# Two VectorE score blocks in one step, and a new plan, in a fused attention and MLP kernel

## The chip, the cores and the metric

The kernel runs on one core of a Trainium2 chip. The metric is the device time of one execution in microseconds (us): the median of several runs. A core has TensorE (PE, with its weight loads shown apart as PEld), VectorE (DVE), ScalarE (ACT), GpSimd (POOL) and SyncE (SP, whose queue starts DMAs). They run side by side and wait for each other on semaphores. TensorE writes its results to PSUM, here eight banks of 128 x 512 float32.

## The reference

The output is a gated mix of two branches over the same input x (2048 x 640, bf16):

```
g = sigmoid(sum(x * gate_w))
a = softmax(q k^T / sqrt(20)) v @ wo        # 32 heads of 20 columns, 2048 x 2048 scores per head
h = x @ w1 + b1                             # 640 -> 1536
b = (h * tanh(softplus(h))) @ w2            # 1536 -> 640
out = g * a + (1 - g) * b
```

The exponentials of the softmax, 32 x 2048 x 2048 of them, are most of the element-wise work.

## The kernel before, in words

**Tiling.** The 2048 queries are cut into four chunks c of 512, the 32 heads into eight groups g of four heads j, the keys into 16 tiles kt of 128. A unit (c, g, kt, j) is one block of scores, 128 keys x 512 queries; there are 2048. The four heads of a group lie on four strips of 32 partitions, so score matmuls (L1163) of different j use different 32-row strips of TensorE and can run at the same time. The last group of chunk 3 is cut into two halves of 256 queries (CUTS). PV matmuls (L1399) take four blocks of one key tile, one per head, and accumulate in PSUM bank 6 (ACC).

**Two ways to an exponential.** ScalarE takes two blocks of a step in one ACTIVATE (`emit_e`, L1190), written to a ring of 16 slots (ETS); with a third block when `third` allows it. VectorE takes whole tiles of four blocks instead: `x_block` picks a tile, a block of it and a bank, `emit_x` issues the block's score matmul and its evacuation (L1248), which turns the score into an integer whose bits are an approximate float16 exponential, in a "line" (LN, or part of HB, REG or W2R). When a tile's four blocks are there, two shaded copies of the line are made (L1278, 128 x 2048), and the three versions go through PV with three scaled copies of V (VS, made by GpSimd at L1303, `weigh`). A VectorE tile so costs four evacuations, two copies and two more PV passes. `start_tile` starts a tile if VectorE's owed work, the free lines and the blocks left in the group allow it; `able` and `room` (with LOAD, GROUP, CALM, LAG, CATCH_UP) gate it from the step loop.

**PSUM.** Banks 0 to 2 and 3 to 5 are the score slots of even and odd steps (`SLOT` = 3). Step s uses the first two banks of its slot; the third of each (2 and 5) and bank 7 are shared (`FLEX`) by VectorE's blocks, by the third block and by the background tasks (`home`). A bank can be taken when its last reader is done in the plan.

**The order of the work** is planned in Python before anything is issued. `Plan` holds a modelled clock for each engine; each `add` puts an instruction behind its engine's last one, with its dependences, which become semaphore waits. The step loop in `attention` runs a step for each exponential of ScalarE: `emit_e(step)`, then the choice of a VectorE block, `compose` (which units ScalarE takes two steps on, by preference on other strips than the VectorE block's), `emit_s`, `emit_x`, PV (`emit_pv`), background tasks (`pick`, `put`) and VectorE's deferred pieces (`work`):

```
x = x_block(step + 2, able) if fast else None
compose(step + 2, x and x[1][3], third(step + 2, x))
emit_s(step + 2)
if x:
    emit_x(step + 2, *x)
```

Background tasks are the projections to Q, K and V, the MLP (`h_task`, evacuated at L941 and blended at L982 to L984; `b_task`, L998) and the output projection (`p_task`, `part_task`, L1021). Each has a due slot (a slot is three blocks, 683 of them, `NSLOT`); those of the MLP and of the output projection of chunks 0 to 2 are spread from `start` (the first block of chunk 2) to `NSLOT - END`. `fill_up` adds matmuls without use (L1685, `spin`), or repeats score matmuls, when the plan's TensorE was busy for less than a share (SPUN, STREAM) of the last WINDOW us; a matmul in flight keeps the clock that TensorE is granted from falling.

A group ends with its last PV; then bank 6 is copied out (L1486), the sums are inverted and spread by DMA, and GpSimd multiplies (L1456).

## Time and profile before

| | |
|---|---|
| median of 3 runs | 770.0 us (768.5 to 771.22) |
| profiled execution: its own time | 769.53 us |
| its span, first to last instruction | 767.7 us |
| mean granted TensorE clock | 0.994 of full |
| DMA | 50.41 MB, mean 66 GB/s |

Durations in the text come from the profiled execution. Two things help to read it. "PE busy" counts matmuls that overlap in a pipeline, so it isn't TensorE's load; a group of matmuls on different strips shows as several records that start within a few ns. And an instruction's duration contains a latency that the next one on the same engine can overlap, so the time that an engine needs per instruction is read from start to start. A row of a view by operation has: line, engine, operation, output <- input, shapes, count | busy us, mean ns of one | idle us just before, and whom that waited for. A row of waits has: who <- whom: us in total, times, longest. A row of the busy time by stretch has: start:end, length, then the busy us (and instructions) of each engine, granted clock, share of the DMA engines busy, GB/s. A timeline row has: start, length, engine, line, operation, count.

### The profile page before, as it was taken

What the parts mean: (1) busy time and instruction counts of PE and PEld (TensorE: products, weight loads), DVE (VectorE), ACT (ScalarE), POOL (GpSimd) and SP (SyncE); (2) the same over time, 40 slices, a digit from 0 to 9 for tenths busy, and PEclk for the clock granted to TensorE, in tenths of its full rate; (3) what the DMA queues carried; (4) which work ended last, traced back from release to release, by engine and by line L of the source; (5) the groups of instructions that cost most, each with busy time, mean ns of one, the idle gap of its engine ahead of it and who ended that gap; (6) DMA issues with size and microseconds to landing.
All of it is one profiled execution on the core that took longest, in us unless ns stands there. A gap on an engine that the chain in (4) does not pass through costs nothing.

```text
span 767.7 us, 25231 instructions
## 1 busy us (share of the span) xinstructions
PE 736.7 (96%) x11185; PEld 277.1 (36%) x11185; DVE 684.9 (89%) x1101; ACT 744.1 (97%) x784; POOL 191.8 (25%) x297
## 2 busy tenths in 40 slices
PE   8999999999999999899999999999999999999995
PEld 3333243333333433223333344433443433332342
DVE  3598899989998999998999899989999999998975
ACT  5999999999999999999999999999999999999994
POOL 3212124223023220223233033311141212324210
PEclk9999999999999999999999999999999999998999
DMA  9423321210234122162212222212222212101001
GB/s 220 70 66 68 100 71 35 64 61 22 73 95 127 54 67 69 51 210 50 59 46 68 58 64 68 51 38 69 66 59 67 66 44 66 34 25 33 16 17 41
DMA packets 78012, 50.41 MB, mean 66 GB/s; under 512 B 21408, under 2 KB 73880, under 8 KB 77848
## 3 DMA queue, kind: packets, MB, share of 16 engines
q1 hardware_dynamic: 75528, 48.24, 23.2%
q8 instruction: 90, 1.47, 0.8%
q10 hardware_dynamic: 2256, 0.47, 0.3%
q0 software_dynamic: 112, 0.01, 0.1%
q14 instruction: 26, 0.21, 0.1%
HBM read 39.01 MB, written 8.90 MB: 62 GB/s over the span
## 4 chain that ended last, share of the span: by engine, by line
ACT 67%; PE 21%; DVE 7%; DMA 3%; SPq 1%; issue 0%
ACT ETS L1190 65%; PE PS L1163 7%; PE PS L1399 6%; PE PS L463 5%; PE PS L807 2%; ACT REG L965 2%; DVE LN L1248 2%; DMA XB<-in_A_x_dram 2%; DVE LN L1278 1%; SPq L512 1%; DMA W2R<-in_B_w_dram 1%; DVE REG L1248 0%; DVE U L983 0%; DVE HB L984 0%; DVE REG L982 0%; PE PS L848 0%
## 5 line engine op out<-in xcount | busy, mean ns | idle before, releaser
L1190 ACT ACTIVATE ETS<-PS 128x1024 bf16<-128x1024 f32 (+1 forms) x753 | 720.9, 1174 | 7.5 <-PE PS L1163 5.9
L1163 PE MATMUL PS<-QT,KT 32*128 32x512 bf16 (+1 forms) x2112 | 295.5, 379 | 17.0 <-ACT ETS L1190 13.8
L1248 DVE TENSOR_SCALAR LN<-PS 128x512 int16<-128x512 f32 x380 | 254.4, 682 | 22.7 <-PE PS L1163 21.4
L1163 PEld LDWEIGHTS PS<-QT,KT 32*128 32x128 bf16 x2112 | 73.9, 91 | 242.6 <-ACT ETS L1190 222.0
L1303 POOL TENSOR_SCALAR VS<-V_all 128x84 bf16<-128x84 bf16 x252 | 140.7, 558 | 83.2 <-DVE V_all L788 34.7
L1456 POOL TENSOR_TENSOR QT<-OUNG,BCT 128x512 bf16<-128x512 f32 x31 | 43.8, 1412 | 465.4 <-DMA BCT<-SUMS 444.8
L1399 PE MATMUL PS<-ETS,V_all 128*21 128x512 bf16 (+1 forms) x1608 | 153.2, 378 | 0.3 <-DVE V_all L788 0.3
L1278 DVE TENSOR_SCALAR LN<-LN 128x2048 int16<-128x2048 int16 x174 | 122.0, 705 | 10.7 <-PE PS L1399 10.1
L463 PE MATMUL PS<-XB,REG 128*32 128x256 bf16 (+1 forms) x1860 | 93.2, 298 | 1.8 <-DMA XB<-in_A_x_dram 0.7
L463 PE MATMUL PS<-W2R,HB 128*32 128x320 bf16 x1536 | 77.2, 302 | 0.2
L1399 PE MATMUL PS<-LN,VS 128*21 128x512 f16 (+1 forms) x784 | 72.9, 377 | 0.6 <-DVE LN L1278 0.6
L1399 PEld LDWEIGHTS PS<-ETS,V_all 128*21 128x21 bf16 x1608 | 39.2, 90 | 61.6 <-issue 55.3
L463 PEld LDWEIGHTS PS<-XB,REG 128*32 128x32 bf16 x1860 | 43.9, 95 | 28.0 <-issue 15.6
L463 PE MATMUL PS<-WOQ,QT 128*32 128x320 bf16 x1024 | 51.4, 300 | 1.2 <-DVE QT L1479 1.2
L463 PEld LDWEIGHTS PS<-W2R,HB 128*32 128x32 bf16 x1536 | 35.8, 96 | 25.4 <-issue 11.7
L1399 PE MATMUL PS<-LN,V_all 128*21 128x512 f16 (+1 forms) x396 | 37.1, 373 | 0.0
L463 PE MATMUL PS<-XB,WOQ 128*32 128x512 bf16 (+2 forms) x440 | 36.5, 382 | 0.0
L941 DVE TENSOR_TENSOR HB<-PS,B1F 128x512 bf16<-128x512 f32 x48 | 32.7, 681 | 0.7 <-PE PS L463 0.4
L1399 PEld LDWEIGHTS PS<-LN,VS 128*21 128x21 bf16 x784 | 17.9, 89 | 37.7 <-issue 22.3
L463 PEld LDWEIGHTS PS<-WOQ,QT 128*32 128x32 bf16 x1024 | 24.4, 96 | 16.2 <-issue 6.3
L1248 DVE TENSOR_SCALAR REG<-PS 128x512 int16<-128x512 f32 x44 | 29.3, 678 | 0.6 <-PE PS L1163 0.4
L1248 DVE TENSOR_SCALAR W2R<-PS 128x512 int16<-128x512 f32 x36 | 24.4, 685 | 4.7 <-PE PS L1163 4.6
(119 smaller groups left out, 517.5 us busy)
## 6 DMA issues: line engine op xcount, KB each, us to landing
REG<-in_B_w_dram SPq DMA_DIRECT2D x36, 320.0 KB, 3.3
BCT<-SUMS SPq DMA_DIRECT2D x31, 256.0 KB
W2R<-in_B_w_dram SPq DMA_DIRECT2D x12, 320.0 KB, 5.7
QT<-QS SPq DMA_DIRECT2D x28, 128.0 KB, 3.4
KT<-KS SPq DMA_DIRECT2D x28, 128.0 KB
KS<-LN SPq DMA_DIRECT2D x16, 128.0 KB, 3.3
QS<-WOQ SPq DMA_DIRECT2D x16, 120.0 KB
W2R<-in_B_w_dram SPq DMA_DIRECT2D x12, 160.0 KB, 3.8
```

The source lines that it names most:

```text
L463: last = e.matmul(to[at + j:at + j + n, :], w[:, j:j + n], x, start=start, stop=stop, tile_position=(0, at + j))
L512: "sp", lambda e: e.dma_start_transpose(xt(c), x_ap[c * CW:(c + 1) * CW, :]), (), f"xt{c}", cost=4.5)]
L807: return lambda e, bank: e.matmul(PS[:, bank, i * n:(i + 1) * n], xt(t // 4)[:, f, t % 4 * P:(t % 4 + 1) * P], WV[:, f, g * HD:g * HD + n] ...
L941: ev = dve(lambda e: e.tensor_tensor(hb, PS[:, bank, :].rearrange("p (i t) -> p i t", i=2), bias, ALU.add), [last, *b1f, *guarded, *b_read ...
L965: ex = pl.add("act", lambda e: e.activation(U, h, AF.Tanh, bias=MXR[:, 3:4], scale=0.5), [ev, u_free[0], m_bias], cost=0.95)
L1163: op = pl.add("pe", lambda e, to=to, g=real(g), tile=tile, j=j, cols=cols, c=c, of_q=of_q: e.matmul(to[:, cols], KT[32 * j:32 * j + 32, g, ...
L1190: e_op[s] = pl.add("act", lambda e: e.activation(RING[:, p:p + n, :], scores(s)[:, 0:n, :], AF.Exp, scale=SCALE), [s_op[s], *(pv_slot[b] f ...
L1248: bank_free[bank] = x_ops[bank] = tile["op"] = dve(lambda e: e.tensor_scalar(dst, PS[:, bank, :], SCALE * ULPS, BASE, ALU.mult, ALU.add), ...
L1278: op = pl.add("dve", lambda e: e.tensor_scalar(to, src, SHADES[n] - SHADES[held], None, ALU.add), [made, *deps], cost=SHADE, port=True)
L1303: weighted[(c, g, k)] = n, [pl.add("pool", lambda e, i=i, n=n, src=src: e.tensor_scalar(VS[:, n, i, :, :], src, WEIGHTS[i + 1], None, ALU. ...
L1399: lasts[n] = pl.add("pe", lambda e, v=v, j=j, src=src[:, cols], of_q=of_q, begin=begin, end=end: e.matmul(PS[32 * j:32 * j + EW, ACC, of_q ...
L1456: oung_free[0] = bc_read[0] = otn_done[(c, g)] = pl.add("pool", lambda e: e.tensor_tensor(otn(c, g), src, BC, ALU.mult), deps, cost=TIMES, ...
```

## The change

A step may take a second VectorE block. After `x_block` has given x, it is called again with `beside` = (x's bank, x's strip). The second call looks at the shared banks other than x's, and gives nothing if VectorE is more than XPAIR = 0.5 us behind ScalarE in the plan or fewer than 32 units are left; otherwise it follows the rules of the first. Its block avoids x's strip if the tile has another one left. `compose` then takes ScalarE's two blocks with both strips marked as used, no third block is allowed, and both are issued, so that the four blocks can lie on four strips.

The plan's numbers are changed too: slack and clearance terms (SLACK, FREE), how far ahead and how late tasks and tiles may be (AHEAD, CATCH_UP, PACKED, ROWED, CALM), the owed work that still lets a tile start (LOAD, GROUP), where the spread background ends (END 75 to 120 slots before the last, SHIFT), and the look back of the fillers (WINDOW).

```diff
-SLACK = 0.219
+SLACK = 0.158
+XPAIR = 0.5
-ROWED = 4
+ROWED = 6
-FREE = 0.209
+FREE = 0.146
-AHEAD = 24
+AHEAD = 26
-CATCH_UP = 372.816
+CATCH_UP = 346.719
-LOAD = 0.823
+LOAD = 0.576
-GROUP = 2.075
+GROUP = 1.453
-END = 75
-SHIFT = 1.348
+END = 120
+SHIFT = 0.944
-WINDOW = 4.9
-CALM = 7
-PACKED = 17
+WINDOW = 3.3
+CALM = 10
+PACKED = 12
...
-        def compose(s, j=None, more=0):
-
-            some, js = [], [j]
+        def compose(s, js=(), more=0):
+
+            some, js = [], list(js)
...
-        def x_block(s, able):
+        def x_block(s, able, beside=None):
...
             homes = [bank for bank in FLEX if bank not in held and not (now["open"] and now["home"] == bank)]
+            if beside:
+                homes = [bank for bank in homes if bank != beside[0]]
+                if max(0.0, pl.now["dve"] - pl.now["act"]) > XPAIR or len(order) < 8 * HG:
+                    return None
...
             js = [v[3] for v in islice(order, HG) if v[:3] == order[0][:3]] if order else []
+            if beside:
+                js = [*js[:1], beside[1]]
             return tile, block_of(tile, js if len(js) <= 2 else []), bank
 
-        def emit_x(s, tile, u, bank):
+        def emit_x(s, tile, u, bank, more=()):
 
             c, g, kt, j = u
-            got = score_mms([(u, PS[:, bank, :])], [bank_free.get(bank), *inputs(u)], [v[3] for v in slots.get(s, ())])
+            got = score_mms([(u, PS[:, bank, :])], [bank_free.get(bank), *inputs(u)], [*more, *(v[3] for v in slots.get(s, ()))])
...
                 x = x_block(step + 2, able) if fast else None
-                compose(step + 2, x and x[1][3], third(step + 2, x))
+                y = x and x_block(step + 2, able, (x[2], x[1][3]))
+                compose(step + 2, [v[1][3] for v in (x, y) if v], 0 if y else third(step + 2, x))
                 emit_s(step + 2)
                 if x:
                     emit_x(step + 2, *x)
+                if y:
+                    emit_x(step + 2, *y, [x[1][3]])
```

## The prediction

> **What bounds the kernel now.** I read the page's totals and chain first, then the busy time of each engine by stretch.
>
> ```profile
> span 767.7 us, 25231 instructions
> ...
> PE 736.7 (96%) x11185; PEld 277.1 (36%) x11185; DVE 684.9 (89%) x1101; ACT 744.1 (97%) x784; POOL 191.8 (25%) x297
> ...
> ACT 67%; PE 21%; DVE 7%; DMA 3%; SPq 1%; issue 0%
> ```
> ```profile
> 20.00:100.00 80.00, 78.26 (x1004) 26.39 (x1001) 65.32 (x111) 79.57 (x88) 13.94 (x27) 1.00 0.32 73
> 100.00:300.00 200.00, 195.79 (x2572) 73.52 (x2573) 184.00 (x308) 197.79 (x209) 50.23 (x83) 1.00 0.23 66
> 300.00:600.00 300.00, 290.19 (x4829) 110.17 (x4824) 280.27 (x432) 299.76 (x311) 75.63 (x111) 1.00 0.25 69
> 600.00:700.00 100.00, 97.86 (x1643) 37.03 (x1631) 98.70 (x152) 99.74 (x109) 26.88 (x36) 1.00 0.16 47
> 700.00:740.00 40.00, 38.48 (x575) 12.77 (x577) 32.84 (x52) 37.42 (x40) 15.28 (x24) 0.91 0.04 12
> ```
>
> The columns of the second view are PE, PEld, DVE, ACT, POOL busy, then the granted clock. ScalarE is full from 20 to 700 us (79.57 + 197.79 + 299.76 + 99.74 of 680, 3.1 us idle), and the chain is mostly its exponentials. VectorE is idle 14.7, 16.0, 19.7, 1.3 and 7.2 us in the five rows, 58.9 in all. So the time falls only if exponentials leave ScalarE, or if its idle time at 700 to 740 us (2.6 us) goes. What it does, and what VectorE takes from it, by operation and form:
>
> ```profile
> L1190 ACT ACTIVATE ETS<-PS 128x1024 bf16<-128x1024 f32 x699 | 660.5, 1142 | 5.3 <-PE PS L1163 4.9 <-PE PS L1399 0.2
> L1248 DVE TENSOR_SCALAR LN<-PS 128x512 int16<-128x512 f32 x380 | 254.4, 682 | 22.7 <-PE PS L1163 21.4
> L1278 DVE TENSOR_SCALAR LN<-LN 128x2048 int16<-128x2048 int16 x174 | 122.0, 705 | 10.7 <-PE PS L1399 10.1
> L1190 ACT ACTIVATE ETS<-PS 128x1536 bf16<-128x1536 f32 x54 | 85.7, 1589 | 2.1 <-PE PS L1399 1.1 <-PE PS L1163 1.0
> L1248 DVE TENSOR_SCALAR REG<-PS 128x512 int16<-128x512 f32 x44 | 29.3, 678 | 0.6 <-PE PS L1163 0.4
> L1248 DVE TENSOR_SCALAR W2R<-PS 128x512 int16<-128x512 f32 x36 | 24.4, 685 | 4.7 <-PE PS L1163 4.6
> L1248 DVE TENSOR_SCALAR HB<-PS 128x512 int16<-128x512 f32 x28 | 18.8, 682 | 2.8 <-PE PS L1163 2.8
> ```
>
> ScalarE takes 2 x 699 + 3 x 54 = 1560 blocks of 128 x 512 and VectorE 380 + 44 + 36 + 28 = 488, together the 2048 that there are. 488 blocks are 122 tiles of four.
>
> **What one tile is worth.** The durations overlap on an engine, so I use start to start, from a run of 20 exponentials and a pair of VectorE's evacuations:
>
> ```profile
> 710.54 18.44 ACT L1190 ACTIVATE ETS<-PS 128x1024 bf16<-128x1024 f32 x20 [0.53 <-PE PS L1163]
> ```
> ```profile
> 723.51 1.28 DVE L1248 TENSOR_SCALAR LN<-PS 128x512 int16<-128x512 f32 x2
> ```
>
> ScalarE: (18.44 - 1.14) / 19 = 0.91 us for two blocks, 0.455 a block, so a tile that leaves it saves 1.82 us. VectorE: 1.28 - 0.68 = 0.60 us a block, and two shaded copies at 0.705: 4 x 0.60 + 1.41 = 3.81 us a tile. A shorter run also takes 1.82 us away from VectorE, so each added tile needs 3.81 + 1.82 = 5.63 us of its idle time.
>
> **The second block (x_block with beside, emit_x twice).** It removes waits of VectorE for a score block: with one block a step it finishes early and the next comes only with the next step's matmuls. The views of who waited for whom, for the whole run and then for 20 to 100 us:
>
> ```profile
> DVE LN L1248 <- PE PS L1163: 21.4, 50, 1.7
> ...
> ACT ETS L1190 <- PE PS L1163: 5.9, 13, 1.0
> ...
> DVE W2R L1248 <- PE PS L1163: 4.6, 6, 1.3
> ...
> DVE HB L1248 <- PE PS L1163: 2.8, 5, 1.9
> ```
> ```profile
> DVE LN L1248 <- PE PS L1163: 4.1, 4, 1.7
> DVE W2R L1248 <- PE PS L1163: 3.3, 4, 1.3
> DVE HB L1248 <- PE PS L1163: 2.8, 5, 1.9
> ```
>
> 28.8 us of VectorE's 58.9 are such waits, and that bounds what pairs can give: 28.8 / 5.63 = 5.1 tiles, 9.3 us. The other end is nothing. 10.2 us of them lie before 100 us, where tiles are few for other reasons (V and K are still being made); 18.6 are left. A pair also needs a second of the three shared banks, while one is held by whatever background task is open, and VectorE at most 0.5 us behind ScalarE in the plan. I take half of the 18.6: 9.3 / 5.63 = 1.65 tiles, **-3.0 us**. With no x block waiting, VectorE's next late item is a shaded copy that waits for PV to give a line back (10.1 us in the L1278 row above), which pairs don't help.
>
> On TensorE a block more in a step costs little, as two groups of score matmuls show:
>
> ```profile
> 431.02 0.39 PE L1163 MATMUL PS<-QT,KT 32*128 32x512 bf16 x4
> 431.94 0.39 PE L1163 MATMUL PS<-QT,KT 32*128 32x512 bf16 x2
> ```
>
> Four blocks on four rows take the 0.39 us of two. A tile's two more PV passes of four matmuls lie in TensorE's waits for ScalarE. The third block of an exponential, which a pair forbids, is worth nothing: 1589 - 1142 = 447 ns against 455, so losing all 54 costs under half a microsecond. What is queued behind a pair is the evacuation of a background task, 0.60 us later; nothing of ScalarE's waits for it, as its own banks are others.
>
> The Trainium skill speaks against the part: the page "TensorEngine Tiling (Array Packing)", section PSUM Bottleneck, says that tiling speeds up TensorE but not the evacuation of PSUM. The trace agrees, since the two evacuations above are serial at 0.60 us each; where VectorE is full (98.70 of 100 us at 600 to 700) a pair is by that rule worth 0, and the sum would then be without the 3.0.
>
> **The shorter look back (WINDOW 4.9 to 3.3).** The fillers at line 1685 exist to keep TensorE's clock up. Once they did not: busy time by 5 us stretches (the last four columns are POOL, clock, DMA share and GB/s), then TensorE's groups before it (first and last of seven), then two groups that run back to back.
>
> ```profile
> 700.00:705.00 5.00, 4.01 (x27) 0.86 (x25) 4.26 (x6) 5.00 (x6) 4.49 (x5) 0.82 0.06 18
> 705.00:710.00 5.00, 5.00 (x45) 1.10 (x44) 2.72 (x4) 3.28 (x4) 3.54 (x6) 0.50 0.01 3
> 710.00:715.00 5.00, 5.00 (x79) 1.61 (x78) 4.09 (x7) 4.47 (x6) 1.59 (x4) 0.99 0.00 0
> ```
> ```profile
> 699.85 0.39 PE L1163 MATMUL PS<-QT,KT 32*128 32x512 bf16 x2
> ...
> 702.84 0.40 PE L1399 MATMUL PS<-ETS,V_all 128*21 128x512 bf16 x4
> ```
> ```profile
> 715.83 0.40 PE L1399 MATMUL PS<-LN,V_all 128*21 128x512 f16 x4
> 716.05 0.39 PE L1399 MATMUL PS<-ETS,V_all 128*21 128x512 bf16 x4
> ```
>
> The clock was halved for 0.18 x 5 / 0.5 + 5 + 0.1 = 6.9 us, and ScalarE lost 1.72 + 0.53 = 2.25 us. Before it, from 699.85 to 703.44 us, seven groups at 0.22 us (716.05 - 715.83) make 1.54 us, 43% occupancy. A look back of 4.9 us still counts denser work from before the lull; one of 3.3 does not, and adds fillers sooner. Bounds: **-2.25 us**, or nothing gained. I take the gain, since the lull is the kind that a shorter mean sees. The page "TensorE: Matmul & The Clock Gate", Part 1, gives a window of about 3.4 us for this gate, which the 6.9 us fit as two, and calls the window that closes it idle; here 43% was enough to close it, and the measurement decides.
>
> **The plan's other numbers.** CALM 7 to 10 starts tiles three slots, 9 blocks, later: at 488 blocks in 753 steps that is 4.5 x 0.65 = 3 blocks, 0.7 tile, 0 to +1.3 us; I take **+0.7**. END 75 to 120 makes the MLP and projection due 45 slots earlier: the work is the same, so 0 where the tail takes the tiles that the middle gives up (rival C below if not). LOAD 0.823 to 0.576 with GROUP allows 0.576 x 1.1 us for each slot left; with 120 left that is 76 us of owed VectorE work, more than remains then once the background is done, so 0. SLACK, FREE, SHIFT, PACKED, ROWED, AHEAD, CATCH_UP reorder work under ScalarE: 0, with 1 us either way as an estimate from the 3.1 us in which ScalarE idles from 20 to 700 us.
>
> **Sum:** -3.0 - 2.25 + 0.7 = -4.55 us on the profiled execution's 769.53 (span 767.7 and 1.8 around it), 765.0. The median of the runs is 0.5 above it, so 765.4.
>
> **Rivals.** The forecast, **A**, spans all waits filled (770 - 9.3 - 2.25 = 758.5) to 767.7.
>
> **B, no change.** Pairs are rarely taken, since a background task holds one of the three banks, or VectorE's idle time is only moved to the shaded copies. For it: 10.1 us of such waits, and 98.70 of 100 us busy late. Against it: the 28.8 us. Tiles stay within one of 122 and the lull comes back in another place: 770, 767.7 to 772.3.
>
> **C, slower: the work that is moved forward is not paid back.** What VectorE does for the background and its densest stretch of tiles (100 to 200 us, lines 1248 and 1190):
>
> ```profile
> L941 DVE TENSOR_TENSOR HB<-PS,B1F 128x512 bf16<-128x512 f32 x48 | 32.7, 681 | 0.7 <-PE PS L463 0.4
> L982 DVE SCALAR_TENSOR_TENSOR REG<-REG 128x1024 f32<-128x1024 f32 x18 | 23.5, 1303 | 1.1 <-ACT REG L965 1.1
> L984 DVE SCALAR_TENSOR_TENSOR HB<-REG,U 128x1024 bf16<-128x1024 f32 x18 | 22.6, 1254 | 0.0
> L983 DVE SCALAR_TENSOR_TENSOR U<-REG,HB 128x1024 f32<-128x1024 f32 x18 | 22.5, 1250 | 0.0
> L998 DVE TENSOR_SCALAR XB<-PS,OMG 128x320 bf16<-128x320 f32 x28 | 15.2, 542 | 1.2 <-PE PS L463 1.2
> ```
> ```profile
> 100.00:200.00 100.00, 51.09 (x77) 1.00 0.18 51
> ```
> ```profile
> 100.00:200.00 100.00, 99.41 (x105) 1.00 0.18 51
> ```
>
> A pair of hidden tasks is 2 x 0.68 + 1.30 + 1.25 + 1.25 = 5.2 us; 18 of them and some 56 small evacuations at 0.54 are 123 us, due over 222 slots where it was 267. At 1.12 us a slot (767.7 / 683) VectorE's share of it rises from 41% to 49%: 8% of 249 us, 20 us or 5 tiles, must move to the tail. The densest stretch so far has 77 / 105 = 0.73 block a step; a VectorE without background could do 0.91 / 0.95 = 0.96, less the groups' own work about 0.9. If the tail stays at 0.73, 55 steps (45 x 1.12 / 0.91) lack 0.17 block each: 9.4 blocks, 2.3 tiles, +4.3 us, and nothing else gained: 774. It decides where the tail's blocks per step stay under 0.9. Against it: that is just where a second block is allowed.
>
> **D, slower by the clock.** In a tail without background TensorE has per step one score group and 0.5 + 0.75 n PV groups for n VectorE blocks: at n = 0.65, 0.22 x 1.99 = 0.44 us of 0.91, 48%; at 0.9, 53%. 43% closed the gate, so it hangs on fillers. Two lulls more than now cost 4.5 us: 774.5.
>
> **How the numbers follow.** A 0.50, B 0.20, C 0.18, D 0.12. This kernel's measurement tells no less than about 0.3% (2.3 us) from no change; by that A is faster, B the same, C and D slower: 0.50, 0.20, 0.30. The time is A's likeliest, 765.4. The range, 758 to 775, goes from A's bound past C and D, with about 1 in 6 left out, mostly above.
>
> **What would show it.** Right: blocks of line 1248 over 488 by 4 to 12 and groups of four score matmuls beside two-block exponentials; VectorE's waits for L1163 near 20 us or under; a clock of 1.00 from 20 to 740 us; ScalarE still full. Wrong: 488 blocks or fewer (B, C; for C fewer from 300 to 600 us and not more after), a halved clock more than once (D), or more than 6 us in which L1190 waits for L1163, which no part of the sum has.

## The result and the profile after

The changed kernel takes **774.3 us** in the median of 14 runs (772.2 to 777.48), where the kernel before, run beside it, takes 770.73 (767.52 to 773.53). The ratio is 1.0045, with a 95% interval of 1.0027 to 1.0063: slower by 0.45%, 3.5 us. The profiled execution took 773.77 us, its span is 772.0, against 769.53 and 767.7. So the profiled executions differ by 4.2 us and show the whole loss.

Two lines of the page of the changed kernel, the totals and the chain that ended last:

```profile
span 772.0 us, 25210 instructions
...
PE 739.4 (96%) x11173; PEld 276.6 (36%) x11176; DVE 687.3 (89%) x1101; ACT 746.5 (97%) x806; POOL 194.1 (25%) x295
...
ACT 50%; PE 31%; DVE 15%; DMA 2%; issue 1%; DVEq 0%; SPq 0%
```

In the chain ScalarE's share fell from 67% to 50%, TensorE's rose from 21% to 31%. The chain is followed back from the last instruction, so this says first that something other than an exponential stands at the end. Busy time by the same stretches as before, and the last 32 us (PE, PEld, DVE, ACT, POOL, then the clock):

```profile
20.00:100.00 80.00, 78.86 (x1026) 27.03 (x1018) 66.65 (x113) 79.68 (x88) 17.90 (x32) 1.00 0.28 73
100.00:300.00 200.00, 195.04 (x2516) 70.99 (x2508) 186.40 (x311) 198.18 (x216) 52.82 (x83) 1.00 0.23 65
300.00:600.00 300.00, 288.57 (x4619) 105.35 (x4612) 281.98 (x439) 298.50 (x321) 78.04 (x115) 1.00 0.24 64
600.00:700.00 100.00, 97.28 (x1672) 38.07 (x1660) 97.29 (x145) 99.25 (x109) 24.32 (x34) 1.00 0.21 59
700.00:740.00 40.00, 38.04 (x639) 14.66 (x640) 32.96 (x52) 39.96 (x44) 12.43 (x17) 1.00 0.06 17
740.00:772.00 32.00, 25.38 (x584) 13.35 (x581) 15.26 (x32) 18.60 (x21) 2.14 (x2) 0.95 0.11 34
```

The last stretch of the kernel before, to its own end:

```profile
740.00:768.00 28.00, 19.16 (x441) 9.43 (x429) 17.01 (x34) 17.64 (x19) 2.52 (x2) 0.94 0.13 38
```

Up to 740 us nothing was lost: ScalarE is as full as before, its idle time at 700 to 740 us is gone (37.42 to 39.96), the clock is 1.00 throughout. The full clock holds for this execution: over the 14, the mean granted clock is 0.991 to 0.999, 0.995 in the median, and 0.998 in the profiled one. The exponentials by form, and VectorE's score blocks:

```profile
L1191 ACT ACTIVATE ETS<-PS 128x1024 bf16<-128x1024 f32 x765 | 711.2, 1119 | 5.0 <-PE PS L1164 4.1
L1255 DVE TENSOR_SCALAR LN<-PS 128x512 int16<-128x512 f32 x376 | 246.7, 678 | 11.9 <-PE PS L1164 11.4
L1255 DVE TENSOR_SCALAR REG<-PS 128x512 int16<-128x512 f32 x56 | 37.2, 680 | 3.3 <-PE PS L1164 3.2
L1255 DVE TENSOR_SCALAR HB<-PS 128x512 int16<-128x512 f32 x32 | 21.2, 681 | 4.2 <-PE PS L1164 4.1
L1191 ACT ACTIVATE ETS<-PS 128x1536 bf16<-128x1536 f32 x10 | 15.3, 1526 | 0.0
L1255 DVE TENSOR_SCALAR W2R<-PS 128x512 int16<-128x512 f32 x24 | 16.0, 680 | 2.4 <-PE PS L1164 2.4
```

376 + 56 + 32 + 24 = 488 blocks, 122 tiles: not one tile more. VectorE's waits for score blocks did fall, from 28.8 to 11.4 + 3.2 + 4.1 + 2.4 = 21.1 us, and counted in the trace, groups of four score matmuls rose from 43 to 91. So pairs are taken, and earlier: 343 of the 488 blocks lie before 500 us, where it was 328. But the last exponential ends at 758.2 us, as before (758.4). ScalarE's last exponentials, before and after:

```profile
751.92 6.46 ACT L1190 ACTIVATE ETS<-PS 128x1536 bf16<-128x1536 f32 x6 [1.08 <-PE PS L1399]
```
```profile
756.20 2.00 ACT L1191 ACTIVATE ETS<-PS 128x1024 bf16<-128x1024 f32 x2
```

**All of the loss of the profiled execution lies behind them:** 9.3 us then, 13.8 us now. Where it comes from shows in two operations of the background, first before, then after (minimum, median and maximum duration in ns, first and last start in us):

```profile
L998 DVE TENSOR_SCALAR XB<-PS,OMG x28: 535/542/552, 380.3 to 734.6; 128x320 bf16<-128x320 f32 x28
...
L1021 DVE SCALAR_TENSOR_TENSOR W2R<-PS,GATE,XB x8: 542/550/551, 737.0 to 756.5; 128x320 f32<-128x320 f32 x8
```
```profile
L999 DVE TENSOR_SCALAR XB<-PS,OMG x28: 531/542/553, 382.7 to 753.1; 128x320 bf16<-128x320 f32 x28
...
L1022 DVE SCALAR_TENSOR_TENSOR W2R<-PS,GATE,XB x8: 540/550/552, 755.7 to 762.9; 128x320 f32<-128x320 f32 x8
```

The first row is the evacuation of the MLP's second product (`b_task`), the second that of the output projection of the last chunk over its first six groups (`part_task`). `part_task` is ready only when all of `b_task` is planned, since it adds to that result and writes over W2's place. The last `b_task` is evacuated 18.5 us later, though END made it due 45 slots earlier, and so of the eight parts, all over by 757.1 us before, six now start behind the last exponential. The chain from there to the output, after and before (start, length, what):

```profile
758.69 4.14 PE PS L464 x116
...
763.46 0.46 PE PS L464 x8
...
763.91 0.46 PE PS L464 x8
...
764.62 1.03 PE PS L464 x24
```
```profile
760.53 0.43 DVE QT L1479
...
761.01 0.48 PE PS L463 x8
```

Before, the end waits for the last group's own normalization (QT at 760.53) and one projection. After, the same normalization is done at 760.47 in the timeline, and the end still has to work through 116 matmuls of parts and the turns of 0.46 us behind them. It is not VectorE that is busy throughout just before: from 740.0 to 758.2 us it is busy for 7.50 us (12.89 before), TensorE for 18.06 (16.82 before), and the late rows of VectorE wait for L464.

### The profile page after: what moved, and what is told of

It reads as the page before. It is cut to its first block, busy times and chain, and to the rows that moved or that the text cites. A ratio compares the mean times of both kernels' runs of the same rounds, so it can differ in the third digit from the quotient of the medians.

```text
span 772.0 us, 25210 instructions
## 1 busy us (share of the span) xinstructions
PE 739.4 (96%) x11173; PEld 276.6 (36%) x11176; DVE 687.3 (89%) x1101; ACT 746.5 (97%) x806; POOL 194.1 (25%) x295
## 4 chain that ended last, share of the span: by engine, by line
ACT 50%; PE 31%; DVE 15%; DMA 2%; issue 1%; DVEq 0%; SPq 0%
ACT ETS L1191 48%; PE PS L1164 11%; PE PS L1406 9%; PE PS L464 8%; DVE LN L1255 5%; DVE LN L1285 3%; PE PS L808 2%; ACT REG L966 1%; PE PS L849 1%; DVE HB L942 1%; DMA RR<-OUNG 1%; DVE U L984 1%; DVE HB L985 1%; DMA LN<-in_A_x_dram 1%; DVE REG L983 1%
## 5 line engine op out<-in xcount | busy, mean ns | idle before, releaser
L1191 ACT ACTIVATE ETS<-PS 128x1024 bf16<-128x1024 f32 x775 | 723.3, 1124 | 5.0 <-PE PS L1164 4.1
L1164 PE MATMUL PS<-QT,KT 32*128 32x512 bf16 (+1 forms) x2114 | 304.1, 378 | 17.5 <-ACT ETS L1191 13.0
L1255 DVE TENSOR_SCALAR LN<-PS 128x512 int16<-128x512 f32 x376 | 246.7, 678 | 11.9 <-PE PS L1164 11.4
L1310 POOL TENSOR_SCALAR VS<-V_all 128x84 bf16<-128x84 bf16 x250 | 144.5, 578 | 91.2 <-DVE V_all L789 26.6
L1164 PEld LDWEIGHTS PS<-QT,KT 32*128 32x128 bf16 x2114 | 75.8, 91 | 251.7 <-ACT ETS L1191 221.4
L1285 DVE TENSOR_SCALAR LN<-LN 128x2048 int16<-128x2048 int16 x176 | 126.2, 721 | 10.6 <-PE PS L1406 9.9
L464 PE MATMUL PS<-XB,REG 128*32 128x256 bf16 (+1 forms) x1860 | 96.4, 298 | 0.8 <-DVE LN L1255 0.6
L464 PE MATMUL PS<-W2R,HB 128*32 128x320 bf16 x1536 | 75.4, 301 | 1.5 <-DVE LN L1255 1.1
L464 PEld LDWEIGHTS PS<-XB,REG 128*32 128x32 bf16 x1860 | 43.3, 95 | 27.9 <-issue 16.9
L464 PE MATMUL PS<-WOQ,QT 128*32 128x320 bf16 x1024 | 48.6, 300 | 0.4 <-issue 0.3
L464 PEld LDWEIGHTS PS<-W2R,HB 128*32 128x32 bf16 x1536 | 35.7, 96 | 25.1 <-issue 11.6
L1255 DVE TENSOR_SCALAR REG<-PS 128x512 int16<-128x512 f32 x56 | 37.2, 680 | 3.3 <-PE PS L1164 3.2
L464 PE MATMUL PS<-XB,WOQ 128*32 128x512 bf16 (+2 forms) x440 | 36.6, 381 | 0.0
L464 PEld LDWEIGHTS PS<-WOQ,QT 128*32 128x32 bf16 x1024 | 24.2, 96 | 14.8 <-issue 6.2
L1493 DVE COPY OUNG<-PS 128x512 f32<-128x512 f32 x31 | 21.2, 684 | 5.6 <-PE PS L1406 5.4
```

Source lines behind the costliest of these rows:

```text
L464: last = e.matmul(to[at + j:at + j + n, :], w[:, j:j + n], x, start=start, stop=stop, tile_position=(0, at + j))
L1164: op = pl.add("pe", lambda e, to=to, g=real(g), tile=tile, j=j, cols=cols, c=c, of_q=of_q: e.matmul(to[:, cols], KT[32 * j:32 * j + 32, g, ...
L1191: e_op[s] = pl.add("act", lambda e: e.activation(RING[:, p:p + n, :], scores(s)[:, 0:n, :], AF.Exp, scale=SCALE), [s_op[s], *(pv_slot[b] f ...
L1255: bank_free[bank] = x_ops[bank] = tile["op"] = dve(lambda e: e.tensor_scalar(dst, PS[:, bank, :], SCALE * ULPS, BASE, ALU.mult, ALU.add), ...
L1285: op = pl.add("dve", lambda e: e.tensor_scalar(to, src, SHADES[n] - SHADES[held], None, ALU.add), [made, *deps], cost=SHADE, port=True)
L1310: weighted[(c, g, k)] = n, [pl.add("pool", lambda e, i=i, n=n, src=src: e.tensor_scalar(VS[:, n, i, :, :], src, WEIGHTS[i + 1], None, ALU. ...
```

## The experiments

How they were read: for each profiled execution I counted VectorE's blocks and took ScalarE's *work* from the first to the last exponential (0.904 us for one of two blocks and 1.330 for one of three, the medians from start to start before, and its other instructions) and its *idle* time, the rest. That rest also holds what exponentials take beyond these medians: of the 19.0 us before, 7.5 are time without a running instruction. *Last W2* is the start of the last `b_task` evacuation, *tail* the time from the end of the last exponential to the end. The next column counts VectorE's instructions in the tail, three of which are in every kernel the branch, the drain and the semaphore of the program's end. *Halved* is the time before the end of the last exponential in which the trace shows TensorE's clock at half.

The ratios are of all executions, the other columns of one, which can lie off the median: it is the slowest with the lull filled (775.89 us, median 770.71), with FREE (783.62, 780.01), with CALM (776.46, 774.74) and with END 75, and the fastest with short parts (771.26, 774.79), with END 90 and with the pair alone and the copy first.

| kernel | ratio to before, 95% | blocks | work + idle | last W2 | last exp. ends | tail | VectorE instr. | halved |
|---|---|---|---|---|---|---|---|---|
| before | | 488 | 728.0 + 19.0 | 734.6 | 758.4 | 9.3 | 12 | 6.8 |
| after | 1.0045 (1.0027 to 1.0063) | 488 | 729.1 + 17.9 | 753.1 | 758.2 | 13.8 | 20 | 0 |
| after, no pair | 1.0102 (1.0063 to 1.0142) | 476 | 734.0 + 14.8 | 747.6 | 759.9 | 12.9 | 19 | 0 |
| pair alone | 1.0152 (1.0117 to 1.0188) | 508 | 720.2 + 27.5 | 764.6 | 758.8 | 20.7 | 26 | 17.1 |
| pair alone, copy first | 1.0136 (1.0077 to 1.0194) | 508 | 720.1 + 23.7 | 760.8 | 755.3 | 20.8 | 26 | 10.2 |
| before, WINDOW 3.3 | 1.0002 (0.9986 to 1.0019) | 488 | 728.0 + 20.8 | 736.1 | 760.3 | 9.3 | 12 | 6.8 |
| before, lull filled | 0.9993 (0.9971 to 1.0015) | 488 | 728.0 + 26.0 | 741.3 | 765.1 | 8.9 | 12 | 13.7 |
| before, CALM 10 | 1.0054 (1.0031 to 1.0076) | 496 | 724.6 + 21.2 | 759.1 | 757.0 | 17.6 | 23 | 6.8 |
| before, FREE .146 | 1.0118 (1.0086 to 1.0149) | 484 | 730.0 + 29.3 | 719.3 | 769.9 | 11.9 | 15 | 30.7 |
| after, END 75 | 1.0096 (1.0064 to 1.0128) | 496 | 725.5 + 26.5 | 759.7 | 763.1 | 14.0 | 20 | 13.7 |
| after, END 90 | 1.0107 (1.0065 to 1.0148) | 496 | 725.9 + 29.0 | 738.0 | 765.7 | 8.8 | 10 | 3.4 |
| after, short parts | 1.0047 (1.0025 to 1.0070) | 488 | 729.1 + 16.3 | 751.6 | 756.7 | 12.8 | 19 | 0 |
| after, thin tail | 1.0010 (0.9996 to 1.0023) | 488 | 729.1 + 17.5 | 752.9 | 758.0 | 12.5 | 19 | 0.3 |
| pair, other numbers | **0.9948** (0.9931 to 0.9965) | 500 | 724.1 + 16.7 | 729.6 | 751.4 | 12.7 | 17 | 0 |
| the same, no pair | 1.0285 (1.0255 to 1.0315) | 500 | 723.4 + 40.3 | 776.5 | 774.3 | 17.2 | 23 | 23.9 |
| the same, copy first | 0.9947 (0.9926 to 0.9968) | 500 | 724.1 + 16.2 | 729.5 | 751.3 | 12.8 | 17 | 0 |
| pair, third numbers | 1.0069 (1.0046 to 1.0092) | 500 | 723.8 + 27.7 | 741.3 | 762.6 | 11.9 | 15 | 13.7 |

Over the table, *idle* goes with *halved*: 14.8 to 17.9 us where at most 0.3 us is halved, 19.0 to 21.2 where 6.8 are, 23.7 to 27.7 from 10.2 to 17.1, 29.3 and 40.3 above. END 90 is the exception, 29.0 us with 3.4. The table doesn't tell which makes the other, a wait that empties TensorE or a halved clock that makes ScalarE wait.

### The pair and the numbers, each without the other

```diff
-XPAIR = 0.5
+XPAIR = -1
```

> The changed kernel with XPAIR = -1: no step takes two VectorE blocks, all other new numbers stay. The planner now hands VectorE 476 blocks instead of 488. Theory (pairs put VectorE's tiles ahead of the background, and what is left of the background after the last exponential is the loss): the background's last W2 evacuation comes earlier than the changed kernel's 753.1 us and the time from the last exponential to the end falls from 13.8 us to about 10; the last exponential comes some 5 us later (12 blocks at 0.455), so the time is about 773 to 777, no gain, but the loss has changed place. Rival N (the new numbers alone make the loss, the pair is harmless): the stretch after the last exponential stays at 13 us or more and the time is 777 or more.

And the other half, the changed kernel with all the old numbers (XPAIR 0.5 stays):

```diff
-SLACK = 0.158
+SLACK = 0.219
...
-FREE = 0.146
+FREE = 0.209
...
-LOAD = 0.576
+LOAD = 0.823
...
-GROUP = 1.453
+GROUP = 2.075
...
-END = 120
-SHIFT = 0.944
+END = 75
+SHIFT = 1.348
...
-WINDOW = 3.3
-CALM = 10
...
+WINDOW = 4.9
+CALM = 7
...
```

> The changed kernel with all numbers of the plan as before the change: the pair alone. The planner hands VectorE 508 blocks (488 before). Theory: ScalarE has 9 us less to do, but the background is done later by about VectorE's time for the 20 added blocks (5 tiles at 3.8 us, 19 us): last W2 evacuation near 750 us or later where it was 734.6, 13 us or more from the last exponential to the end where it was 9.3, and a time of 773 to 780, slower than before. Rival N: the pair pays as forecast, 762 to 767.

Measured: 776.81 us without the pair, 781.53 with the pair alone, against 770.61 beside them. Both halves are slower than before, and each is slower than the two together. Without the pair the new numbers cost 12 blocks (ScalarE's work rises by 6.0 us, its idle time falls by 4.2) and 3.6 us of tail. That tail of 12.9 us is a miss: about 10 was expected, and 13 or more was the sign of the rival, by which the new numbers alone make the loss. They do make most of the longer tail without any pair. On them the pair wins the 12 blocks back, 4.9 us of work, and 0.57% in the two ratios; a part of the 0.57% is clock, since three of the seven executions without the pair show 0.985 and take 781 to 783 us. With a clock of 0.995 or more the means are 775.6 (four executions) and 773.9 with the pair (ten), 1.7 us. On the old numbers the pair wins 20 blocks, five tiles, 7.8 us of ScalarE's work, and loses more: ScalarE idles 8.5 us more and the tail is 11.4 us longer; the signs are those that were expected, the time is 1.5 us above the range. Two rows of waits of the kernel with the pair alone:

```profile
ACT ETS L1191 <- PE PS L1164: 9.0, 21, 1.1
ACT ETS L1191 <- PE PS L1406: 5.2, 5, 2.0
```

In the kernel before these two rows have 5.9 and 1.3 us. The row of the chain:

```profile
759.53 11.58 PE PS L464 x302
```

302 matmuls of the MLP's second product and of the output projection stand between the last exponential and the end. VectorE's idle time from 20 to 740 us fell only from 58.9 to 47.2, where five tiles at 5.63 us are 28 us. Counted without overlaps, evacuations and copies for the tiles took 15.9 us more in that stretch: 11.6 came out of idle time, the other 4.3 are background that VectorE did not do in it.

### The clock

```diff
-WINDOW = 4.9
+WINDOW = 3.3
```

> The kernel before with WINDOW = 3.3 in place of 4.9 and nothing else. VectorE's and ScalarE's instructions come out the same, in the same order; on TensorE a few fillers move by some groups. The prediction gave the shorter look back 2.25 us, by taking away the halved clock at 703 us. If that holds: clock 1.00 from 690 to 715 us and 768 to 769. Theory now (the lull is a stall of that plan, and fillers in the look back's reach do not cover it): no change, 769.5 to 772, and ScalarE still waits 2 us or more between 700 and 725 us.

And the fillers by force: the score matmuls of the steps at the lull are issued twice.

```diff
-            s_op[s] = score_mms([...], deps)
+            s_op[s] = score_mms([...], deps, times=1 + (fast and 690 <= s <= 706))
```

> The kernel before with the same plan, but the score matmuls of steps 690 to 706 (about 693 to 712 us) are issued twice, so that TensorE is some 65% occupied where it was 43%. If the halved clock at 703 to 710 us cost ScalarE its 2.25 us there: granted clock 1.00 over 690 to 715 us, ScalarE full there, and 767.5 to 769, 1 to 2.5 us under the kernel before. If the stall came from the group's end instead and the clock only followed it: the same idle time of ScalarE and no gain, or a loss of up to 1 us from the added matmuls.

Measured: 771.31 us beside 771.61, and 770.71 beside 770.61: no change in either. Busy time by 5 us stretches, first with WINDOW 3.3 alone, then with the doubled matmuls:

```profile
700.00:705.00 5.00, 2.64 (x28) 0.71 (x25) 3.15 (x6) 4.01 (x5) 2.39 (x3) 0.83 0.17 59
705.00:710.00 5.00, 4.67 (x30) 0.91 (x33) 2.38 (x3) 3.07 (x3) 4.44 (x8) 0.50 0.02 3
```
```profile
705.00:710.00 5.00, 3.57 (x21) 0.61 (x22) 3.96 (x5) 3.29 (x4) 4.60 (x6) 0.71 0.08 21
710.00:715.00 5.00, 5.00 (x39) 0.96 (x38) 1.93 (x3) 2.51 (x3) 2.59 (x6) 0.50 0.00 0
```

With WINDOW 3.3 the lull is there, with 0.83 and 0.50 in the two stretches, where it was 0.82 and 0.50 before, and over the 12 executions the clock is 0.990 to 0.995, as beside them. The shorter look back does not remove it.

With the doubled matmuls the answer is less clear. In the profiled execution the lull is longer and some us later, and 21 matmuls in 5 us show that TensorE had little ready to run. But this is the slowest of 12, with a clock of 0.990. Over the twelve it is 0.996 in the median, against 0.993 in the 22 executions beside them, and six have 0.997 or 0.998. So the lull is probably shorter or absent in many of them, and no trace of such a one was kept. The median is the same all the same, so what the clock wins there the doubled matmuls seem to cost elsewhere: those six take 769.8 us in the mean, and the three executions of the kernel before with 0.997 or 0.998 take 767.1 to 768.6.

What the clock goes with in time shows in the 87 executions of the kernel before that ran beside the experiments. In the mean, 5 with 0.990 take 772.8 us, 34 with 0.993 take 771.1, 14 with 0.995 take 769.8, and 4 with 0.999 take 767.6. The profiled execution of the changed kernel has no lull before the last exponential; since WINDOW alone leaves it, it is something else in that plan. What starts it in the old plan, and what takes it away in the new one, stays open.

### One number alone

```diff
-CALM = 7
+CALM = 10
```

> The kernel before with CALM = 10 in place of 7 and nothing else: no pair; tiles start three slots later. The forecast of the prediction for this number was +0.7 us. Theory (tail set by the background's end, whatever moved it): the planner hands VectorE 496 blocks and puts the last W2 evacuation behind the last exponential's neighbourhood, so a tail of 13 to 17 us and 775 to 780. Rival N2 (only the pair moves the background): within 2 us of the kernel before.

```diff
-FREE = 0.209
+FREE = 0.146
```

> The kernel before with FREE = 0.146 in place of 0.209 and nothing else: VectorE gets 484 blocks, and the background's last W2 evacuation comes some 20 us earlier than in the kernel before. Theory: a tail of about 9 us is the floor (last PV, normalisation, last projections, stores), so the earlier background gains nothing there, and the four blocks fewer put the last exponential 1 to 2 us later: 770 to 773. Rival F (an earlier background keeps shortening the tail): tail under 8 us and 768 or less.

Measured: 774.74 and 780.01 us beside 770.70, so +4.2 and +9.1 us by the ratios, from one number of the plan each. CALM gives eight blocks *more* and a tail of 17.6 us; FREE gives an early background (719.3) and late exponentials (769.9), with ScalarE's row of waits at

```profile
ACT ETS L1190 <- PE PS L1163: 15.2, 22, 1.8
```

where it was 5.9. CALM's signs are about those expected; FREE's time is a miss of 7 us, and its tail is 11.9 where 9 was expected. FREE's added idle time goes with the clock: in its profiled execution five halved stretches, 30.7 us, lie before the last exponential, where the kernel before has 6.8. Of the time in which ScalarE runs nothing, 10.5 of 15.5 us lie in them, against 1.8 of 7.5. Each choice of the plan depends on all before it, so one other choice early gives another plan throughout.

### END: pushed late, or exchanged

```diff
-END = 120
+END = 75
```

> The changed kernel with END back at 75, everything else new: the MLP and projections are due 45 slots later again. Theory (the background ends late because VectorE takes tiles first, wherever its due times lie): the last W2 evacuation stays near 750 (753.1 in the changed kernel, 734.6 before), the tail after the last exponential stays at 12.5 to 15 us, and the median within 4 us of 774. Rival (the new END itself pushed the background to the end): the last W2 evacuation goes back to 735 to 740, the tail to 9 to 10.5 us, and the median to 768 to 771.

```diff
-END = 120
+END = 90
```

> The changed kernel with END 90. By the first theory nothing sets in between and it looks like the changed kernel: last W2 evacuation 748 or later, tail over 12 us. A third theory: the end of the background and the end of the exponentials are exchanged for each other, since both want VectorE and TensorE; then a kernel with an early last W2 evacuation (735 to 740) and a short tail (9.5 to 11 us by the count of what is left) has its last exponential later, at 763 or more, and is no faster than 774.

Measured: 778.43 and 777.93 us beside 769.50. With END 75 the background does not come back to 735: the last W2 evacuation is at 759.7, the tail 14.0. So the new END did not push it late. The theory's sizes were a little short: the evacuation comes 9.7 us later than the 750 that was expected, and the median is 0.4 us beyond the 4 us allowed. With END 90 the background is early, as two rows of its VectorE show, and ScalarE waits instead:

```profile
L999 DVE TENSOR_SCALAR XB<-PS,OMG x28: 535/550/552, 382.2 to 738.0; 128x320 bf16<-128x320 f32 x28
...
L1022 DVE SCALAR_TENSOR_TENSOR W2R<-PS,GATE,XB x8: 541/550/552, 740.9 to 760.1; 128x320 f32<-128x320 f32 x8
```
```profile
ACT ETS L1191 <- PE PS L1406: 10.7, 7, 1.9
```

The tail is 8.8 us, shorter than before, and the last exponential ends at 765.7, 7.3 us later than before. That is as the third theory has it: the end of the background and the end of the exponentials are exchanged. The table is no proof of it. FREE (719.3 and 769.9) and the third set (741.3 and 762.6) also have the background early and the exponentials late, and CALM (759.1 and 757.0) and the pair alone (764.6 and 758.8) the reverse. But FREE's late exponentials go with its halved clock, and with END 75 and with the first set without the pair both ends come late (759.7 and 763.1, 776.5 and 774.3). So the exchange is not shown as a rule.

### What the tail consists of

The first kernel leaves out matmuls of `part_task` (all but the first and the last group), the second also narrows the last chunk's parts and rests to 8 of 320 columns; the plan is that of the changed kernel in both.

```diff
-            return Task([p_mm(c, t, half, g, early) for g in early], HALF * COL, finish, due, ready)
+            return Task([p_mm(c, t, half, g, early) if g in (early[0], early[-1]) else lambda e, bank: None for g in early],
+                        HALF * COL, finish, due, ready)
```

> The changed kernel with the same plan, but of the six groups that the eight partial output projections of the last chunk add up, only the first and the last are multiplied (so the last 512 rows of the output are not the reference's). Theory: the last exponential ends at about 758 as in the changed kernel; of the 148 projection matmuls after it some 60 to 80 are missing, at 0.158 us for four that is 2.4 to 3.2 us, so the time falls to about 771.5. Rival S (ScalarE's lost third blocks and waits make the loss, the matmuls after the last exponential are covered by the last group's normalisation and the stores): within 1 us of the changed kernel.

```diff
...
-                dst, PS[:, bank, 0:HALF], GATE[:, tb:tb + 1], add, ALU.mult, ALU.add), [*deps, *gate_done], HALVED)
+                dst[:, 0:n], PS[:, bank, 0:n], GATE[:, tb:tb + 1], add[:, 0:n], ALU.mult, ALU.add), [*deps, *gate_done], HALVED)
...
```

> The changed kernel with the same plan, but the small tasks that finish the last chunk (eight partial output projections, four remainders) work on 8 of 320 columns, matmul and VectorE evacuation alike, and the partial ones on the first and last of their six groups only (so the last 512 rows of the output are not the reference's). Fewer matmuls alone (r3_short_parts) left 19 VectorE instructions after the last exponential and did not shorten the run. Theory (the tail is a queue of these tasks, each paying an evacuation on VectorE of 0.47 us and a turn of a bank): the last exponential stays near 757 to 758, the stretch after it falls from 13.8 us to 9.5 to 11.5, the time from 774.3 to 770 to 772. Rival S (the tail is set by the last group's normalisation and the stores, and is long in the changed kernel for another reason): tail 12.5 us or more, time within 1.5 us of the changed kernel.

Measured: 774.79 us beside 770.61 for the first, so nothing won, a miss; 772.15 beside 771.61 for the second, where the ratio goes from 1.0045 to 1.0010, 2.7 us. The chain of the first kernel tells why:

```profile
758.80 0.47 DVE W2R L1022
...
759.31 0.46 PE PS L464 x8
...
759.77 0.46 PE PS L464 x8
```

Without the matmuls it is the evacuations that go one after another, a turn each 0.46 us: two limits of about the same length stand behind each other. Only with both thinned does most of the loss go, 2.7 of 3.5 us, although the twelve executions have a lower clock (0.988 to 0.994) than those of the changed kernel. The profiled tail does not show this size: it falls from 13.8 to 12.5 us, where 9.5 to 11.5 was expected, and the clock is halved in it from 757.6 to 764.5 us. So these small tasks carry most of the loss; what each of them costs stays open. The Trainium skill has this as a caution, in the page "TensorEngine Tiling (Array Packing)", section PSUM Bottleneck: faster TensorE work may leave the evacuation of PSUM as the limit. The trace agrees, at 0.46 us a turn. The tail goes with the count of VectorE's instructions in it over all runs: 10 or 12 make 8.8 to 9.3 us, 15 make 11.9, 17 to 20 make 12.5 to 14.0, 23 make 17.2 to 17.6, 26 make 20.7 to 20.8.

### The pair with numbers of its own

Two other sets of numbers, chosen by the plan's own modelled clock with the pair allowed; the first, in part, against the changed kernel:

```diff
-SLACK = 0.158
+SLACK = 0.219
...
-XPAIR = 0.5
+XPAIR = 0.2
...
-FREE = 0.146
+FREE = 0.209
...
-LOAD = 0.576
+LOAD = 0.75
...
-GROUP = 1.453
+GROUP = 2.671
...
-END = 120
-SHIFT = 0.944
+END = 70
+SHIFT = 1.155
...
-CALM = 10
-PACKED = 12
...
+CALM = 5
+PACKED = 17
...
```

> The pair on, with another set of the plan's numbers (XPAIR 0.2, END 70, SHIFT 1.155, CALM 5, LOAD 0.75, GROUP 2.671, ROWED 3, BUSY 0.976 and smaller moves of a dozen others), for which the planner hands VectorE 500 blocks and sets the last W2 evacuation about as early as in the kernel before. Theory (the pair's tiles are worth ScalarE's time, and the loss is the background that is left after the last exponential): last W2 evacuation 20 us or more ahead of the last exponential, a tail of 9 to 10 us as in the kernel before, the last exponential 0 to 4 us earlier than its 758.4, so 765 to 771. Rival W (a pair costs ScalarE waits in every plan, because it stands in front of evacuations that TensorE needs): ScalarE's idle time from first to last exponential 5 us or more above the 19 us of the kernel before, last exponential at 758 or later, 770 or more.

> The numbers of s1_pair_searched with XPAIR = -1: no pair. The planner hands VectorE 500 blocks here too. If the pair were harmful by itself, taking it away would gain: 770 or less. Theory (each set of numbers fits one order of the work, and what counts is how far ahead of the last exponential the background ends): the background's last W2 evacuation is some 20 us later than with the pair, less than 10 us from the last exponential, the tail 13 us or more, and the time 775 to 784.

The second set has XPAIR 0.3, END 75, SHIFT 0.87, CALM 7, AHEAD 101, CATCH_UP 28.655 and others:

> The pair on with a third set of numbers (XPAIR 0.3, END 75, SHIFT 0.87, CALM 7, BUSY 0.435, AHEAD 101 and others), for which the planner hands VectorE 500 blocks, as in s1_pair_searched, with the background's end at about the same place. Theory (with 500 blocks and a background that ends 20 us ahead of the last exponential the pair gains): last exponential 751 to 755, tail 9.3 to 13, time 763 to 769, under the kernel before. Rival (s1_pair_searched is one lucky order of the work, and the pair as such gives nothing): 770 or more.

Measured: **766.27 us** with the first set, beside 770.70, faster than both kernels; 792.33 with the same numbers and no pair, 8 us above what was expected; 776.67 with the second set, beside 771.61, a miss of some 8 us. Where the first set stands, in its page's first line, its waits and its VectorE:

```profile
span 764.1 us, 25320 instructions
```
```profile
ACT ETS L1191 <- PE PS L1164: 4.3, 11, 0.7
ACT ETS L1191 <- PE PS L1406: 0.3, 1, 0.3
```
```profile
L999 DVE TENSOR_SCALAR XB<-PS,OMG x28: 533/540/552, 381.8 to 729.6; 128x320 bf16<-128x320 f32 x28
...
L1022 DVE SCALAR_TENSOR_TENSOR W2R<-PS,GATE,XB x8: 539/541/551, 736.1 to 755.0; 128x320 f32<-128x320 f32 x8
```

500 blocks, three tiles more than before, ScalarE's idle time 2.3 us less, the background done *earlier* than before. Nothing is exchanged here: the last exponential and the last W2 evacuation both come sooner (751.4 and 729.6), and 3.4 us of longer tail (12.7 where 9 to 10 was expected) are all it gives back. But the tail takes back most of the 3.9 us that ScalarE's work falls by, and the 2.3 us of idle time are about what the prediction has for the lull (2.25), which the first set doesn't have. Its twelve executions have a clock of 0.997 to 0.999; the five of the kernel before with 0.998 or 0.999 take 767.5 us in the mean, so at a like clock some 1 us of the gain is left. That the gain is the pair's, and not that of a plan without a lull, is not shown: no other set of numbers without the pair was searched and run. Without the pair the same numbers lose 26 us: ScalarE waits 22.2 us for score matmuls, and 23.9 us are halved. That their first choices then lead elsewhere is argued, not shown. So neither XPAIR nor a number has a price of its own.

### Is it the accumulator's copy?

With the pair alone 5.6 of ScalarE's 13.2 us of waits from 20 to 758 us lay within 6 us after a copy of bank 6 (L1493), which can stand behind x blocks on VectorE (the 7.0 in the expectation has one more wait, of 1.3 us, which ends as the copy starts). The copy is moved ahead of VectorE instructions that were not needed by it, four times with the old numbers, three with the first set:

```diff
+        for op in self.copies:
+            ready = max(d.t1 + HOP for d in op.deps)
...
+                self.ops.insert(i, self.ops.pop(k))
```

> The second block with all old numbers, as in the run of the pair alone, with the same choices of the plan; only VectorE's order is changed: at 4 of the 31 group ends the copy of the accumulator (line 1493 there, 0.6 us) goes ahead of the x evacuation that stood before it. If ScalarE's extra waits under pairs come from the copy standing behind x blocks (7.0 of the 13.2 us of waits between 20 and 758 us lay within 6 us after such a copy), each move takes about 0.6 us of wait away and spares the clock lull that follows at some of them: ScalarE idle 27.5 to 22..25 us and a median of 777 to 780 against 781.5. Rival: the waits come from what the plan of that kernel does anyhow (TensorE behind, score matmuls late), and the copy only stands near them: idle stays within 1 us of 27.5 and the median within 1.5 us of 781.5. In both the tail after the last exponential stays at 20 us, as its tasks are the same.

> The fastest set of numbers so far (766.3), with the same order change at 3 group ends. In its trace only 0.3 us of ScalarE's waits lay near such copies, so by the first theory there is almost nothing to gain: 765.5 to 767. By the rival also no change. It tells whether the order of the copy is a gain by itself in a kernel whose waits are already gone; 764 or less would speak for a cause that neither has.

Measured: 779.50 us beside 771.06 (ratio 1.0136, its interval overlaps that of the pair alone), and 766.17, no change. The first kernel's totals lie in the ranges of the theory (idle 23.7 us); the places do not bear it out. ScalarE at two of the copies, first with the pair alone, then with the copy first:

```profile
339.55 1.94 ACT L1191 ACTIVATE ETS<-PS 128x1024 bf16<-128x1024 f32 x2 [2.00 <-PE PS L1406]
```
```profile
338.98 1.94 ACT L1206 ACTIVATE ETS<-PS 128x1024 bf16<-128x1024 f32 x2 [1.39 <-PE PS L1421]
```
```profile
621.32 1.02 ACT L1206 ACTIVATE ETS<-PS 128x1024 bf16<-128x1024 f32 x1 [1.44 <-PE PS L1421]
```

At the first place the wait falls by the expected 0.6 us, from 2.00 to 1.39. At the second it was 1.44 and stays 1.44. Within 6 us after copies there are still 4.6 us of waits. The copy's place explains about 1 of 5.6 us; 2.3 of the 3.8 us by which the idle time fell lie after 750 us, where the clock was halved with the pair alone and not in this run. Of the rest, 3.2 us are waits for PV and 1.4 for score matmuls, and what holds these up there stays open.

## Why the prediction was wrong, point by point

**The forecast, 765.4, faster.** It came out 8.9 us higher, slower, within the range of 758 to 775. Two steps failed: the sum holds the stretch behind the last exponential fixed, and this grew from 9.3 to 13.8 us; and the waits that pairs take from VectorE were turned into 1.65 tiles, where not one tile came.

**The second block, -3.0 us.** The mechanism is real: pairs are taken, TensorE's busy time is about the same (736.7 and 739.4 us), and VectorE's waits fell to 21.1 us as "near 20 us or under" had it. The step that failed is "each added tile needs 3.81 + 1.82 = 5.63 us of its idle time", by which waits taken away become tiles. A tile comes when the plan starts it, whatever the idle time. With the pair alone, five tiles cost 11.6 us of idle time from 20 to 740 us and not 28, 4.3 us of background moved out of that stretch, and the tail grew by 11.4 us. That VectorE's tiles are what made the background late is argued: from 740 us to the last exponential it is TensorE that is busy throughout, and VectorE is not. In the changed kernel 7.7 us less of waits for score blocks gave no tile at all, and some of it turned up as waits for late background, as for the MLP's second product, 1.2 us before:

```profile
L999 DVE TENSOR_SCALAR XB<-PS,OMG 128x320 bf16<-128x320 f32 x28 | 15.2, 543 | 6.1 <-PE PS L464 5.9
```

**The shorter look back, -2.25 us.** The clocks above bear out about such a size for a lull, the mechanism was wrong. "one of 3.3 does not, and adds fillers sooner" is undone by WINDOW alone (1.0002) with the same lull at the same place. In the profiled execution the lull did go, so the sign looked right for the wrong reason: "a clock of 1.00 from 20 to 740 us" cannot tell a better filler from another plan. At a like clock the loss is a little larger than it looks: with 0.995 the kernel before takes 769.8 us in the mean, the changed one 773.9.

**CALM, +0.7.** Its sign came true and its reason didn't: alone it gives blocks instead of costing them, and loses 4.2 us, with a tail of 17.6 us against 9.3.

**"Reorder work under ScalarE: 0, with 1 us either way", and END 0.** This is the largest miss of the sum. FREE alone is +9.1 us, END 75 or 90 in the changed kernel +0.5 and +0.6% on top of its 1.0045, and all new numbers without the pair +7.9 us by their ratio, where the sum had -1.55. The 3.1 us of ScalarE's idle time are no bound for what a reordering can do: it can add idle time (29.3 us with FREE where it was 19.0, with the clock halved for 30.7 us) and it can put work behind the last exponential.

**No term for the tail.** The sum treated the last 9 us as fixed. Its signs show it: clock, waits, groups of four and ScalarE full up to 740 us all came out as for "right", only the count of blocks spoke against, and the loss lay where no sign looked.

**The rivals.** C gave 774 and 774.3 was measured, which is luck, since its mechanism was not seen: it wanted fewer blocks from 300 to 600 us, not paid back late. The trace has more blocks by 500 us and fewer late (20 instead of 29 from 700 to 750 us); it is the background that came late. C was right that work moved in time need not be paid back, and had the two kinds of work exchanged. D did not happen: no lull up to 768.9 us, and over all executions the clock is no lower than before (0.995 and 0.993 in the median). B's blocks did stay at 488, while the time did not.

**The third block, "worth nothing".** From start to start an exponential of three blocks takes 1.330 us, against 1.5 x 0.904 = 1.356: 26 ns each, not 8, taken from durations. 44 of them lost are the 1.1 us by which ScalarE's work rose. Small, and hidden by the lull that went.

## What to carry to other kernels

Ask of every edit to an order not only what the bound engine saves but what is still undone when it has finished: count the small tasks left, and the dependence that lets them start, and price them by the turn of the engine that drains them. A new freedom for one engine can be paid by whatever else that engine, or the next one, has to do; where a plan made of greedy choices decides that, a price for one constant can't be read from the profile. Plans with the pair took from 766.2 to 781.5 us here, and the kernel before 770.7. Compare at a like clock before a gain is put down to the change. A sign that would look the same under another cause (a lull that is gone) proves nothing until the cause is tried alone.

## What the runs showed of the hardware

In all 17 traces the halved clocks before the last exponential came in stretches of 3.4, 6.8 or 10.2 us. With FREE alone one lasted 10.2 us, and ScalarE got 7.62 us of work into it:

```profile
723.20:733.40 10.20, 9.22 (x72) 1.91 (x72) 5.24 (x10) 7.62 (x8) 0.00 (x0) 0.50 0.02 3
```

The Trainium skill's page "TensorE: Matmul & The Clock Gate", Part 1, gives a free running window of 3.413 us, of which 10.2 are three, and the runs agree.

A shaded copy on VectorE that meets GpSimd's multiplication of 128 x 512 takes longer. Two rows of the kernel before, VectorE's and GpSimd's:

```profile
700.80 1.15 DVE L1278 TENSOR_SCALAR LN<-LN 128x2048 int16<-128x2048 int16 x1
```
```profile
700.13 1.27 POOL L1456 TENSOR_TENSOR QT<-OUNG,BCT 128x512 bf16<-128x512 f32 x1 [15.18 <-DMA BCT<-SUMS]
```

The multiplication ends at 701.40 and the copy 0.55 us after it; over the trace 18 of 244 copies overlap one and took 1.00 us in the mean, the others 0.69. Who began first decides: nine of the 18 began before the multiplication and took 0.68 to 0.70 us, eight began in the middle of one and ended 0.55 us after it. The Trainium skill's page "SBUF — State Buffer", section Who interferes with whom, says that the two engines share a pair of ports, which the one that issues first holds for its whole instruction. The row agrees: the copy runs when the other is done.
